# q of the first four pairs loaded in two DMAs of 2 KB rows, and a planner fed with traced landing times

## The chip, the cores and the metric

The kernel runs on one core of one Trainium2 chip. The metric is the device time of one execution in microseconds (us). The time before is the median of three runs.

## The reference

The inputs are q, k and v of shape (8, 8, 576, 64) (batch, heads, positions, head size) and two weights, w_in (512 x 2048) and w_out (2048 x 512), all fp32. The first half is retention, which is attention without a softmax and with a decay that depends on the head:

```python
scores = scale * np.matmul(q, k.transpose(0, 1, 3, 2))
gamma = 1.0 - 2.0 ** (-5.0 - np.arange(H, dtype=np.float32))
Dmat = np.where(rel >= 0, gamma[:, None, None] ** rel[None, :, :], 0.0)
ret = scores * Dmat[None, :, :, :]
return np.matmul(ret, v).astype(np.float32)
```

The second half takes the result as 4608 tokens of 512 and computes relu(x @ w_in) squared, times w_out. The output is 4608 x 512 in fp32.

## The kernel before

**Tiles.** The work is cut into 36 units of 128 tokens (all heads): 32 full ones (one batch entry, one chunk c of 128 positions) and four tail ones, which put the last 64 positions of two batch entries together. Two units make a group, so there are 18 groups. Each group has a retention part and a feed-forward part. Retention of a chunk is computed as scores inside the chunk (psc, masked into rx or rT), sums of k and v (psS) that go into a running state R, and an output psO, which takes the masked scores and the state of the chunk before. The decay is put into v (vdec), into R (dec128) and into the output (gam_full). The result is xT, in fp16. The feed-forward part multiplies xT with w_in into ph (L876), takes relu (rl) and square (gT) on ScalarE or VectorE, and multiplies gT with w_out into po. From group 1 on this second product is done by Strassen's scheme: seven half-size products (L973) over sums gS of gT (L946, VectorE) and differences wT of w_out (L827, VectorE). Group 0 uses w_out as it is (L916).

**The first four pairs.** Units 0 to 7 (PAIRED = 8) are handled as pairs of 256 positions of one batch entry. For these k, q and v are each loaded in one DMA (add_load_pair, L308) into a tile "pair" of 128 partitions, 8 heads and 128 numbers; a partition holds two consecutive positions (e = 0, 1), so that a row in memory has 2 x 64 fp32 numbers, 512 bytes. The casts to fp16 (L424; for v L420, with the decay) bring e out again, TensorE transposes k and q in blocks (psT, L439), and ScalarE or VectorE copy them to kqT (L450). Which engine casts what is set at L411. Positions of even and odd number sit apart in kqT, so the mask of the pairs (mask2, L211) and the product that forms xT (L577) are indexed by e. The later units load q in rows of 1 KB (L298) and are transposed by a DMA.

**The front.** FIRST (L240) sets the order of the first transfers: k0, q0, v0, k2, q2, v2, then the eight weight blocks w0 to w3 (w_in) and w4 to w7 (w_out), then k4, q4, v4, k6, q6, v6. The pair loads are issued by SyncE. The weight blocks are issued by GpSimd (L331), which casts them to fp16 on the way: the first issue waits for v0 to land, and the load of k4 waits for w5. The tile of a pair load comes from the pool "stage" (tag "wst", four buffers), which also holds gS. Until the first ph, TensorE has little to do; a list of 34 matmuls on zeros ("warm", WARM at L225) fills what the planner sees as idle time.

**The order of the work.** Every piece of work is a task with an engine, a key (priority), a duration, dependencies and resources. Schedule.emit (L42) plays these through in modelled time: each engine takes the ready task of the lowest key, and the order in which the tasks start is the order in which instructions are written into the engines' queues. On the chip each engine then works in this fixed order and waits on semaphores. The durations and landing times in the model thus cost nothing themselves, but they set the order. LAG holds extra landing time of single transfers (k4 and q4 only). BESIDE is a longer duration for the second half of a sum that is expected to collide with GpSimd. The constants of the tail units are made by tail_pool (L275), whose gate is tied to the cast of unit 4; unit 4 is one of a pair and has no such gate, so they are made at the very start.

Of the kernel before, what the change touches and what calls it, by code (L numbers as in the profile page):

```python
# [15 lines left out]
class Schedule:  # L16
# [7 lines left out]
    def add(self, eng, key, dur, fn, deps=(), acq=(), after=None, lag=0.0):  # L24
        t = dict(eng=eng, key=key, dur=dur, fn=fn, acq=acq, n=len(self.tasks), users=[], free=[], lag=lag,
                 left=len(deps), ready=0.0, lat=self.LAT[eng] if after is None else after)
        for d in deps:
            d["users"].append(t)
        self.tasks.append(t)
        return t  # L30
# [11 lines left out]
    def emit(self):  # L42
        ready = {e: [] for e in self.LAT}
        busy = {e: False for e in self.LAT}
        events = []
        order = []
        seq = 0

        def push(at, what, t):
            nonlocal seq  # L50
            seq += 1
            heapq.heappush(events, (at, seq, what, t))
        for t in self.tasks:
            if t["left"] == 0:
                heapq.heappush(ready[t["eng"]], (t["key"], t["n"], t))
        now = 0.0
        while True:
            for e in ready:
                if busy[e]:
                    continue  # L60
                held = []
                while ready[e]:
                    item = heapq.heappop(ready[e])
                    t = item[2]
                    if all(self.count[r] >= t["acq"].count(r) for r in t["acq"]):
                        for r in t["acq"]:
                            self.count[r] -= 1
                        t["start"] = now
                        order.append(t)
                        busy[e] = True  # L70
                        push(now + t["dur"], "end", t)
                        break
                    held.append(item)
                for item in held:
                    heapq.heappush(ready[e], item)
            if not events:
                break
            now = events[0][0]
            while events and events[0][0] <= now + 1e-9:
                _, _, what, t = heapq.heappop(events)  # L80
                if what == "end":
                    busy[t["eng"]] = False
                    for w in t["users"]:
# [20 lines left out]
def kernel(  # L104
# [9 lines left out]
    nc = tc.nc  # L114
# [96 lines left out]
    mask2 = const.tile([P, 2, 2, 64], FP32, name="mask2")  # L211
    nc.gpsimd.memset(mask2, 1.0)
    for c in range(2):
        for e in range(2):
            m = mask2[c * 64:(c + 1) * 64, e]
            nc.gpsimd.affine_select(out=m, in_=m, compare_op=ALU.is_ge, fill=0.0, base=-e, pattern=[[1, 2], [2, 64]],  # L216
                                    channel_multiplier=-2)
# [12 lines left out]
    BESIDE = 1.1  # L230
# [6 lines left out]
    LAG = {"k4": 0.7, "q4": 0.5}  # L237
# [37 lines left out]
    tail_pool = add_gated("POOL", 4, "v", 2.2, make_tail_pool)  # L275
# [32 lines left out]
    def add_load_pair(name, u):  # L308
        n = "kqv".index(name)

        def fn():
            if name != "q":
                tile_of["stage", u] = stage.tile([P, 2, H, 2 * D], FP32, name="pair", tag="wst")
            x = tile_of[name + "32", u] = tile_of["stage", u][:, n % 2]
            b, c = units[u][1:]
            t = nc.sync.dma_start(out=x, in_=(k, q, v)[n][b, :, c * P:(c + 2) * P, :].rearrange("h (p e) d -> p h (e d)", e=2))
            if (name, u) == ("k", 4):
                behind(t, tile_of["w", 5])
            tile_of["load", name, u] = t
        loaded[name, u] = loaded[name, u + 1] = dma_task(0, 1.81 if loaded else 2.9, fn, acq=("wst",) if name != "q" else (),  # L320
# [4 lines left out]
    def add_weight(i):  # L325
# [10 lines left out]
        t = add("SP", 0, 2.75, lambda: None, deps=last_load + [issue], after=2.1 + LAG.get(f"w{i}", 0.0))  # L336
# [25 lines left out]
    def half(x):  # L362
        return slice(64 * x, 64 * x + 64)
# [39 lines left out]
    def add_unit_pair(u, base):  # L403
# [4 lines left out]
        for i, name in enumerate("kqv"):  # L408
            xs[name] = []
            for e in range(2):  # L410
                eng = ("DVE" if (e if name == "v" else lead) else "ACT" if name == "k" and u >= 4 or u == 2 and e else  # L411
                       "DVE" if name == "q" and u == 2 else "POOL")

                def fc(name=name, e=e, eng=eng):
# [4 lines left out]
                    if name == "v":  # L419
                        (nc.vector if eng == "DVE" else nc.gpsimd).tensor_tensor(  # L420
                            out=t.rearrange("p (h d) -> p h d", d=D), in0=x,
                            in1=vdec[f"pair{e}"].rearrange("p (h o) -> p h o", o=1).to_broadcast([P, H, D]), op=ALU.mult)
                    else:
# [10 lines left out]
        for i, name in enumerate("kq"):  # L434
# [9 lines left out]
            for s in range(2):  # L444
                on_act = i == 0 or s == 0 or u > 0

                def fe(i=i, s=s, on_act=on_act):
                    if i == 0:
                        tile_of["kqT", u + s] = work.tile([P, 2 * NP, P], FP16, name="kqT", tag="kqT", bufs=6)
                    (nc.scalar.copy if on_act else nc.vector.tensor_copy)(  # L450
                        out=tile_of["kqT", u + s][:, i * NP:(i + 1) * NP].rearrange("p x (e t) -> p e x t", e=2),
                        in_=tile_of["psT", u, i][:, :, :, half(s)])
# [15 lines left out]
    def add_ret_pair(g):  # L468
# [7 lines left out]
        for e in range(2):  # L476
# [11 lines left out]
            for a in range(2):  # L488
                def fm(e=e, a=a):
                    nc.vector.tensor_tensor(  # L490
                        out=rT[e][:, a], in0=rT["ps", e][a].rearrange("p (n i) -> p n i", i=P),
                        in1=mask2[:, e].rearrange("p (o e) i -> p o (e i)", o=1).to_broadcast([P, NP, P]), op=ALU.mult)
# [208 lines left out]
    def after_sums(g, t, key, res):  # L701
# [24 lines left out]
        r2 = add("DVE", key + 0.3, 0.65, fr2, deps=[r1], acq=("R",))  # L726
# [95 lines left out]
    def add_wT(i, in0, in1):  # L822
        ts = []
        for h in range(2):
# [3 lines left out]
            ts.append(add("DVE", WT_KEY + i, 0.7, f, deps=sum((wcast[j] for j in range(4, 8 if i else 6)), [])))  # L828
# [6 lines left out]
    for x, y in ((t2, t1), (t4, t2)):  # L835
        for p in y:
            for w in x:
                sched.need(w, p)
# [19 lines left out]
    def add_ff(g):  # L858
# [10 lines left out]
        for fb in range(NF // nf):  # L869
# [18 lines left out]
            def fg(fb=fb, on_act=on_act):  # L888
# [43 lines left out]
    def add_strassen(g, us, base, sq):  # L932
# [7 lines left out]
        def add_sum(k, key, parts, in0, in1, op, deps, start=()):  # L940
            out_ = []
            for h in range(parts):
# [4 lines left out]
                out_.append(add("DVE", key + h, (BESIDE if h else 0.5) if parts > 1 else 0.8, f, deps=deps(h, parts) + list(start)))  # L947
# [164 lines left out]
```

## Time and profile before

| | before |
|---|---|
| median of 3 runs | 289.68 us (289.43 to 289.87) |
| span of the profiled execution | 288.5 us |
| TensorE matmul busy | 280.7 us |
| ScalarE busy | 187.5 us |
| VectorE busy | 177.7 us |
| GpSimd busy | 87.1 us |
| read from memory, written | 36.70 MB, 9.44 MB |
| share of ph (L876) in the chain that ended last | 43% |
| share of po (L973) in it | 36% |
| share of the DMA of w_in in it | 3% |

The profile is of one execution. Busy time is the time in which an engine works on an instruction; matmuls are pipelined, so a busy TensorE isn't always at its peak. The chain that ended last is followed back from the last instruction, at each step to what released it. In the profile's names PE is TensorE (PEld its weight loads), DVE is VectorE, ACT is ScalarE, POOL is GpSimd and SP is SyncE.

### The profile page before, as it was taken

Reading aid. Unit: us, or ns where it says so; the run is one execution under the profiler, and the core shown is the slowest. Engines: PE = TensorE matmul, PEld = TensorE weight load, DVE = VectorE, ACT = ScalarE, POOL = GpSimd, SP = SyncE. Lnnn points to the kernel's source line nnn. Section 1 sums busy time; section 2 is a strip of 40 time slices with the busy share of each in tenths; the row PEclk is TensorE's granted clock in tenths of the full one; section 3 lists DMA queues with packets and bytes.
Section 4 is the critical chain, followed back from the end, with each engine's and each line's share of the span. In section 5 each row is a group of like instructions: output and inputs, shape, how many; then the busy total and the mean of one; then the engine's idle time right before and its main releaser. Section 6 shows DMA issues by size and latency. Waiting matters only on the chain.

```text
span 288.5 us, 10135 instructions
## 1 busy us (share of the span) xinstructions
PE 280.7 (97%) x4346; PEld 236.0 (82%) x4346; DVE 177.7 (62%) x341; ACT 187.5 (65%) x363; POOL 87.1 (30%) x124
## 2 busy tenths in 40 slices
PE   7999999999999999999999999999999999999994
PEld 2568767888888888888888888888888888888883
DVE  3772389868466756657666574767666566364632
ACT  5558975667584757667575748675848665847830
POOL 5660045433525243423325151534433100000000
PEclk9999999999999999999999999999999999999999
DMA  7999999999999898989898997989899420102004
GB/s 202 275 208 206 248 277 267 168 240 144 212 222 186 210 201 216 179 214 168 222 146 197 231 185 182 220 200 248 177 160 228 110 75 5 73 2 75 0 2 145
DMA packets 122156, 49.94 MB, mean 173 GB/s; under 512 B 94720, under 2 KB 117760, under 8 KB 122112
## 3 DMA queue, kind: packets, MB, share of 16 engines
q1 hardware_dynamic: 117568, 44.84, 71.0%
q0 software_dynamic: 4224, 4.19, 8.8%
q8 instruction: 34, 0.56, 0.8%
q10 hardware_dynamic: 320, 0.26, 0.4%
q14 instruction: 10, 0.08, 0.1%
HBM read 36.70 MB, written 9.44 MB: 160 GB/s over the span
## 4 chain that ended last, share of the span: by engine, by line
PE 88%; DMA 3%; DVE 3%; POOL 2%; issue 2%; DVEq 0%; POOLq 0%
PE ph L876 43%; PE po L973 36%; PE psO L357 4%; DMA w_in<-in_moe_w_in_dram 3%; PE po L916 2%; PE psS L357 2%; PE psc L357 2%; DVE rx L490 1%; DVE o L996 1%; DVE gS L946 1%; POOL mask L216 0%; DVE vx L420 0%; POOL vx L420 0%; POOL w_in L331 0%; PE psT L439 0%
## 5 line engine op out<-in xcount | busy, mean ns | idle before, releaser
L876 PE MATMUL ph<-xT,w_in 128*128 128x256 f16 x1152 | 136.6, 273 | 0.3 <-DMA w_in<-in_moe_w_in_dram 0.3
L876 PEld LDWEIGHTS <-w_in 128*128 128x128 f16 x1152 | 111.4, 98 | 14.7 <-DMA w_in<-in_moe_w_in_dram 0.6
L884 ACT ACTIVATE rl<-ph 128x512 f16<-128x512 f32 x144 | 84.3, 586 | 50.7 <-PE ph L876 48.1
L894 ACT ACTIVATE gT<-rl 128x512 f16<-128x512 f16 x118 | 74.4, 631 | 3.4
L973 PEld LDWEIGHTS <-gS 128*128 128x128 f16 x544 | 51.7, 98 | 6.5
L973 PE MATMUL po<-wT,gS 128*128 128x256 f16 x408 | 55.8, 273 | 0.0
L946 DVE TENSOR_TENSOR gS<-gT,gS 128x512 f16<-128x512 f16 (+1 forms) x51 | 31.3, 613 | 24.2 <-ACT gT L894 23.7
L973 PEld LDWEIGHTS <-gT 128*128 128x128 f16 x408 | 39.6, 98 | 4.8
L973 PE MATMUL po<-w_out,gT 128*128 128x256 f16 x272 | 36.8, 273 | 0.0
L387 POOL TENSOR_TENSOR v<-v,vdec_full 128x512 f16<-128x512 f32 x24 | 26.6, 1108 | 28.1 <-DMA v<-in_v_dram 24.4
L371 POOL CAST kq<-k 128x512 f16<-128x512 f32 x28 | 19.7, 702 | 36.9 <-DMA k<-in_k_dram 31.2
L946 DVE TENSOR_TENSOR gS<-gT 128x1024 f16<-128x1024 f16 x34 | 24.7, 726 | 6.4 <-ACT gT L894 6.3
L382 POOL CAST kq<-q 128x512 f16<-128x512 f32 x24 | 15.6, 649 | 32.0 <-DMA q<-in_q_dram 31.8
L896 DVE TENSOR_TENSOR gT<-rl 128x512 f16<-128x512 f16 x26 | 11.8, 455 | 20.1 <-ACT rl L884 20.1
L996 DVE TENSOR_TENSOR o<-po,u 128x256 f32<-128x256 f32 x33 | 13.9, 422 | 15.3 <-PE po L973 7.7
L986 ACT COPY u<-po 128x256 f32<-128x256 f32 x34 | 12.5, 368 | 15.7 <-PE po L973 15.5
L751 DVE TENSOR_TENSOR xT<-psO,gam_full 128x512 f16<-128x512 f32 x28 | 18.0, 685 | 3.8 <-PE psO L357 3.6
L996 DVE TENSOR_TENSOR o<-po,p 128x256 f32<-128x256 f32 x18 | 7.6, 424 | 20.6 <-ACT u L986 12.7
L973 PE MATMUL po<-w_out,gS 128*128 128x256 f16 x136 | 18.0, 273 | 0.0
L692 DVE TENSOR_TENSOR rT<-psc,mask_full 128x512 f16<-128x512 f32 x24 | 15.6, 685 | 3.7 <-PE psc L357 3.2
L973 PE MATMUL po<-wT,gT 128*128 128x256 f16 x136 | 17.6, 273 | 0.0
L1047 ACT COPY o<-po 128x256 f32<-128x256 f32 x16 | 5.9, 370 | 10.8 <-PE po L973 9.1
(82 smaller groups left out, 227.1 us busy)
## 6 DMA issues: line engine op xcount, KB each, us to landing
out_dram<-o SPq DMA_DIRECT2D x32, 256.0 KB, 3.0
k<-in_k_dram SPq DMA_DIRECT2D x24, 256.0 KB, 4.5
q<-in_q_dram SPq DMA_DIRECT2D x96, 64.0 KB, 3.2
v<-in_v_dram SPq DMA_DIRECT2D x24, 256.0 KB, 3.5
pair<-in_k_dram SPq DMA_DIRECT2D x4, 512.0 KB, 7.0
pair<-in_q_dram SPq DMA_DIRECT2D x4, 512.0 KB, 6.1
pair<-in_v_dram SPq DMA_DIRECT2D x4, 512.0 KB, 6.6
w_in<-in_moe_w_in_dram POOLq DMA_DIRECT2D x4, 512.0 KB, 9.2
```

The lines of the kernel that those rows point to most:

```text
L357: t = nc.tensor.matmul(out_, lhsT=lhsT, rhs=rhs, start=start, stop=True, skip_group_check=True, tile_position=(64 * row, 64 * col))
L371: op(out=out_.rearrange("p (n b a d) -> p n b a d", n=2, b=2, a=2), in_=in_.rearrange("p (a n b) d -> p n b a d", n=2, a=2))
L382: nc.gpsimd.tensor_copy(out=tile_of["kq", u][:, 1].rearrange("p (t a d) -> p a t d", t=4, a=2), in_=tile_of["q32", u].rearrange("p (a t) d ...
L387: nc.gpsimd.tensor_tensor(out=t, in0=tile_of["v32", u], in1=vdec[kind].rearrange("p (h o) -> p h o", o=1).to_broadcast([P, H, D]), op=ALU. ...
L692: tile_of["masking", g] = nc.vector.tensor_tensor(out=tile_of["rT", g][:, :, a], in0=tile_of["psc", g][a].rearrange("p (s n i) -> p s n i" ...
L751: nc.vector.tensor_tensor(out=tile_of["x", g].rearrange("p n (s e i) -> p e (n s) i", s=n, e=2)[:, c], in0=y.rearrange("p (o t r) -> p o r ...
L876: nc.tensor.matmul(tile_of["ph", g, fb][:, j, :], lhsT=w_in16[:, m, fi * P:(fi + 1) * P], rhs=tile_of["x", g][:, m, :], start=(m == 0), st ...
L884: nc.scalar.activation(out=t, in_=tile_of["ph", g, fb], func=ACTF.Relu)
L894: nc.scalar.activation(out=t, in_=rl, func=ACTF.Square)
L946: nc.vector.tensor_tensor(out=tile_of["S", g][:, k, sl], in0=in0(sl), in1=in1(sl), op=op)
L973: nc.tensor.matmul(tile_of["pb", g, bank], lhsT=left(i), rhs=right[:, i, :], start=(start and i == 0), stop=(i == HF - 1), skip_group_chec ...
L996: nc.vector.tensor_tensor(out=o_tile(u)[:, half * HM:(half + 1) * HM], in0=bank(x), in1=tile_of[name, g], op=ALU.add)
```

## The change

It has four parts. First, q of each of the four pairs is loaded in two DMAs (heads 0 to 3 and 4 to 7), where a partition takes eight consecutive positions of one head, so that a row in memory has 2 KB. The positions then lie in another order, which the q casts, the copies to kqT, mask2 and the product for xT follow: position 8r + t of a chunk in place of 2i + e. Second, the two casts of k and the two of q in the pair of units 2 and 3 all go to ScalarE, and the tail's constants are tied to unit 8. Third, the planner gets landing times as traced (LAG for 13 transfers, 3.0 in place of 2.1 us for the weights, 2.58 in place of 2.75 us for each one's place in the stream, 1.41 in place of 1.81 for q). Fourth, the planner learns that some VectorE operations ("soft") run slowly while GpSimd works on something longer than 0.5 us (rate SHARED = 0.22), with shorter durations for these when they run alone; the halves of wT depend only on the halves they read; and HURRY brings forward the last relu, the squares on VectorE and the sums of group 1. The number of fillers, 34, is not changed by the diff.

```diff
@@ the planner
+    SHARED = 0.22
-    def add(self, eng, key, dur, fn, deps=(), acq=(), after=None, lag=0.0):
+    def add(self, eng, key, dur, fn, deps=(), acq=(), after=None, lag=0.0, soft=False):
...
+        def shared(beside):
+            t = port["task"]
+            if t is not None:
+                port["left"] -= (now - port["at"]) * (self.SHARED if port["beside"] else 1.0)
+                port["at"] = now
+                t["end"] = now + max(port["left"], 0.0) / (self.SHARED if beside else 1.0)
+                push(t["end"], "end", t)
+            port["beside"] = beside
...
+                        if e == "POOL" and t["dur"] > 0.5:
+                            shared(True)
...
@@ constants
-    mask2 = const.tile([P, 2, 2, 64], FP32, name="mask2")
+    mask2 = const.tile([P, 2, 8, 16], FP32, name="mask2")
...
-    BESIDE = 1.1
+    HURRY = 60
-    LAG = {"k4": 0.7, "q4": 0.5}
+    LAG = {"k0": 0.3, "q0": 0.6, "v0": 0.3, "k2": 0.2, "q2": 0.5, "v2": 1.0, "w2": 0.7, "w7": 1.4, "k4": 0.3, "q4": 1.1, "v4": 0.9, "q6": 0.8, "v6": 0.2}
-    tail_pool = add_gated("POOL", 4, "v", 2.2, make_tail_pool)
+    tail_pool = add_gated("POOL", 8, "v", 0.45, make_tail_pool)
@@ loads
-            t = nc.sync.dma_start(out=x, in_=(k, q, v)[n][b, :, c * P:(c + 2) * P, :].rearrange("h (p e) d -> p h (e d)", e=2))
+            src = (k, q, v)[n][b, :, c * P:(c + 2) * P, :]
+            if name == "q":
+                for a in range(2):
+                    t = nc.sync.dma_start(out=x[:, NP * a:NP * a + NP].rearrange("p t d -> p (t d)"),
+                                          in_=src.rearrange("(a x) (r t) d -> a r x (t d)", a=2, t=8)[a])
+            else:
+                t = nc.sync.dma_start(out=x, in_=src.rearrange("h (p e) d -> p h (e d)", e=2))
-        loaded[name, u] = loaded[name, u + 1] = dma_task(0, 1.81 if loaded else 2.9, fn, acq=("wst",) if name != "q" else (),
+        loaded[name, u] = loaded[name, u + 1] = dma_task(0, 2.9 if not loaded else 1.41 if name == "q" else 1.81, fn, acq=("wst",) if name != "q" else (),
-        t = add("SP", 0, 2.75, lambda: None, deps=last_load + [issue], after=2.1 + LAG.get(f"w{i}", 0.0))
+        t = add("SP", 0, 2.58, lambda: None, deps=last_load + [issue], after=3.0 + LAG.get(f"w{i}", 0.0))
@@ casts, copies, products of a pair
-                eng = ("DVE" if (e if name == "v" else lead) else "ACT" if name == "k" and u >= 4 or u == 2 and e else
-                       "DVE" if name == "q" and u == 2 else "POOL")
+                eng = ("DVE" if (e if name == "v" else lead) else "ACT" if name == "k" and u >= 4 or u == 2 and name != "v" else "POOL")
+                    elif name == "q":
+                        x = tile_of["q32", u].rearrange("p (a t) (s d) -> p a (t s) d", a=2, s=2)[:, :, NP * e:NP * e + NP]
+                        engines[eng](out=t.rearrange("p (t a d) -> p a t d", t=NP, a=2), in_=x)
...
+                        out_ = out_.rearrange("p x (t r) -> p t x r", r=16)
+                        in_ = in_.rearrange("p e y (r x) -> p (e y) x r", x=NP)[:, :, :, 16 * s:16 * s + 16]
...
-                    out=tile_of["x", g][:, :, s * P:(s + 1) * P].rearrange("p n (i e) -> p n e i", e=2),
-                    in0=tile_of["psO", g][s].rearrange("p (n e i) -> p n e i", n=NP, e=2),
-                    in1=gam_f.rearrange("p n (i e) -> p n e i", e=2), op=ALU.mult)
+                    out=tile_of["x", g][:, :, s * P:(s + 1) * P].rearrange("p n (r t) -> p n r t", t=8),
+                    in0=tile_of["psO", g][s].rearrange("p (n t r) -> p n r t", n=NP, t=8),
+                    in1=gam_f.rearrange("p n (r t) -> p n r t", t=8), op=ALU.mult)
@@ state, wT, squares, sums
-        r2 = add("DVE", key + 0.3, 0.65, fr2, deps=[r1], acq=("R",))
+        r2 = add("DVE", key + 0.3, 0.62, fr2, deps=[r1], acq=("R",), soft=True)
-            ts.append(add("DVE", WT_KEY + i, 0.7, f, deps=sum((wcast[j] for j in range(4, 8 if i else 6)), [])))
+            ts.append(add("DVE", WT_KEY + i, 0.68, f, deps=wcast[4 + h] + (wcast[6 + h] if i else []), soft=True))
-            r = add("ACT", place(4 * fb + 4), 0.6, fr, deps=[f1[-1]], acq=("rl",))
+            r = add("ACT", place(4 * fb + 4) - HURRY * (g == 1 and fb == 7), 0.6, fr, deps=[f1[-1]], acq=("rl",))
-            sq.append(add("ACT" if on_act else "DVE", place(4 * fb + 6), 0.63 if on_act else 0.55, fg, deps=[r] + sq[:1],
-                          acq=() if fb else ("g",)))
+            sq.append(add("ACT" if on_act else "DVE", place(4 * fb + 6) - HURRY * (g == 1 and not on_act), 0.63 if on_act else 0.43, fg, deps=[r] + sq[:1],
+                          acq=() if fb else ("g",), soft=not on_act))
-                out_.append(add("DVE", key + h, (BESIDE if h else 0.5) if parts > 1 else 0.8, f, deps=deps(h, parts) + list(start)))
+                out_.append(add("DVE", key + h - HURRY * (g == 1), 0.43 if parts > 1 else 0.72, f, deps=deps(h, parts) + list(start), soft=True))
```

More of the change, by code (lines that the diff above doesn't have):

```diff
@@ L22, in __init__ @@
         self.tasks = []
-    def add(self, eng, key, dur, fn, deps=(), acq=(), after=None, lag=0.0):
-        t = dict(eng=eng, key=key, dur=dur, fn=fn, acq=acq, n=len(self.tasks), users=[], free=[], lag=lag,
+    SHARED = 0.22
+    def add(self, eng, key, dur, fn, deps=(), acq=(), after=None, lag=0.0, soft=False):
+        t = dict(soft=soft, eng=eng, key=key, dur=dur, fn=fn, acq=acq, n=len(self.tasks), users=[], free=[], lag=lag,
                  left=len(deps), ready=0.0, lat=self.LAT[eng] if after is None else after)
@@ L56, in emit @@
         now = 0.0
+        port = dict(task=None, left=0.0, at=0.0, beside=False)
+        def shared(beside):
[6 more added lines that the diff above has]
+            port["beside"] = beside
         while True:
@@ L70, in emit @@
                         busy[e] = True
-                        push(now + t["dur"], "end", t)
+                        t["end"] = now + t["dur"]
+                        if t["soft"]:
+                            port.update(task=t, left=t["dur"], at=now)
+                            shared(port["beside"])
+                        else:
+                            push(t["end"], "end", t)
+                        if e == "POOL" and t["dur"] > 0.5:
+                            shared(True)
                         break
@@ L81, in emit @@
                 if what == "end":
+                    if abs(t["end"] - now) > 1e-6:
+                        continue
+                    t["end"] = -1.0
                     busy[t["eng"]] = False
+                    if t["soft"]:
+                        port["task"] = None
+                    elif t["eng"] == "POOL" and t["dur"] > 0.5:
+                        shared(False)
                     for w in t["users"]:
@@ L215 @@
             m = mask2[c * 64:(c + 1) * 64, e]
-            nc.gpsimd.affine_select(out=m, in_=m, compare_op=ALU.is_ge, fill=0.0, base=-e, pattern=[[1, 2], [2, 64]],
+            nc.gpsimd.affine_select(out=m, in_=m, compare_op=ALU.is_ge, fill=0.0, base=-e, pattern=[[1, 8], [8, 16]],
                                     channel_multiplier=-2)
@@ L315, in fn @@
             b, c = units[u][1:]
-            t = nc.sync.dma_start(out=x, in_=(k, q, v)[n][b, :, c * P:(c + 2) * P, :].rearrange("h (p e) d -> p h (e d)", e=2))
+            src = (k, q, v)[n][b, :, c * P:(c + 2) * P, :]
[3 more added lines that the diff above has]
+                                          in_=src.rearrange("(a x) (r t) d -> a r x (t d)", a=2, t=8)[a])
+            else:
+                t = nc.sync.dma_start(out=x, in_=src.rearrange("h (p e) d -> p h (e d)", e=2))
             if (name, u) == ("k", 4):
@@ L449, in fe @@
                         tile_of["kqT", u + s] = work.tile([P, 2 * NP, P], FP16, name="kqT", tag="kqT", bufs=6)
-                    (nc.scalar.copy if on_act else nc.vector.tensor_copy)(
-                        out=tile_of["kqT", u + s][:, i * NP:(i + 1) * NP].rearrange("p x (e t) -> p e x t", e=2),
-                        in_=tile_of["psT", u, i][:, :, :, half(s)])
+                    out_, in_ = tile_of["kqT", u + s][:, i * NP:(i + 1) * NP], tile_of["psT", u, i]
+                    if i == 0:
+                        out_, in_ = out_.rearrange("p x (e t) -> p e x t", e=2), in_[:, :, :, half(s)]
+                    else:
+                        out_ = out_.rearrange("p x (t r) -> p t x r", r=16)
+                        in_ = in_.rearrange("p e y (r x) -> p (e y) x r", x=NP)[:, :, :, 16 * s:16 * s + 16]
+                    (nc.scalar.copy if on_act else nc.vector.tensor_copy)(out=out_, in_=in_)
                 es.append(add("ACT" if on_act else "DVE", base + 3 + i + s / 2, 0.66, fe, deps=[t] + T["kqT", u + s],
@@ L491, in fm @@
                         out=rT[e][:, a], in0=rT["ps", e][a].rearrange("p (n i) -> p n i", i=P),
-                        in1=mask2[:, e].rearrange("p (o e) i -> p o (e i)", o=1).to_broadcast([P, NP, P]), op=ALU.mult)
+                        in1=mask2[:, e].rearrange("p (o t) r -> p o (t r)", o=1).to_broadcast([P, NP, P]), op=ALU.mult)
                 ms.append(add("DVE", base + 5 + e, 0.66, fm, deps=[t] + ms))
@@ L835 @@
     for x, y in ((t2, t1), (t4, t2)):
-        for p in y:
-            for w in x:
-                sched.need(w, p)
+        for w, p in zip(x, y):
+            sched.need(w, p)
     wT_done = {7: t3, 6: t2, 5: t1, 4: t4}
```

## The prediction

> **What bounds the kernel now.** I read the page first, for the engines and the slices.
>
> ```profile
> PE 280.7 (97%) x4346; PEld 236.0 (82%) x4346; DVE 177.7 (62%) x341; ACT 187.5 (65%) x363; POOL 87.1 (30%) x124
> ...
> PE   7999999999999999999999999999999999999994
> ...
> DMA  7999999999999898989898997989899420102004
> ```
>
> TensorE is busy in 97% of the span, and no other engine passes 65%. The matmuls aren't changed in number or shape, so the time can only come from stretches in which TensorE waits, or does fillers. The slices show one such stretch at the front (the 7) and one at the end (the 4). The DMA row is near 9 from the second slice to the 32nd, so at the front the transfers are the suspect. The chain of waits, in order of time, says which transfer:
>
> ```profile
> 8.90 0.98 POOL w_in L331
> 9.95 0.99 POOL vx L420
> 10.94 8.99 DMA w_in<-in_moe_w_in_dram
> 19.97 1.48 PE ph L876 x12
> 21.46 0.68 PE psO L357 x40
> 22.24 0.31 PE psO L357 x8
> 22.54 5.78 PE ph L876 x52
> ```
>
> The second block of w_in, issued at 10.94 us, lands at 10.94 + 8.99 = 19.93, and the ph matmuls wait for it. Behind that the chain runs on TensorE almost without a break to 43. What happens before 19.93 matters only through this landing. TensorE by microsecond:
>
> ```profile
> 18.00:19.00 1.00, 1.00 (x12) 1.00 1.24 205
> 19.00:20.00 1.00, 0.68 (x7) 1.00 1.24 208
> 20.00:21.00 1.00, 1.00 (x10) 1.00 1.25 206
> ...
> 48.00:49.00 1.00, 0.92 (x52) 1.00 0.65 167
> 49.00:50.00 1.00, 0.69 (x27) 1.00 1.26 287
> 50.00:51.00 1.00, 1.00 (x35) 1.00 1.09 224
> ```
>
> Busy time is the second figure: 0.32 us is idle at 19 to 20 (this is the wait for w_in) and 0.31 us at 49 to 50, where psS waits for VectorE's vx. There is little more to win after 20 us than these two. Last, why w_in lands when it does. First the transfers of 5 to 9 us, then the queues in 12 to 13 us:
>
> ```profile
> DMA packets 2299, 1.16 MB, mean 290 GB/s; under 512 B 32, under 2 KB 2299, under 8 KB 2299
> ...
> q1 hardware_dynamic: 2299, 1.16, 119.7%
> ```
>
> ```profile
> q1 hardware_dynamic: 552, 0.28, 114.9%
> q0 software_dynamic: 9, 0.01, 5.4%
> ```
>
> The six loads of the first two pairs (k0, q0, v0, k2, q2, v2; 0.524 MB each, in rows of 512 B) go at 290 GB/s, 1.81 us each. The first weight block was issued at 8.89 us, yet only 9 packets of its queue had moved before 13 us: it stands behind the pair loads. From there the stream is full, and the blocks land at 17.43, 19.93 and 22.43, 2.5 us apart. So each microsecond saved in the pair loads brings every weight block forward by as much.
>
> **What the Trainium skill says.** "DMA: Bandwidth & Descriptors", section "Specifications", gives a fabric ceiling of 435 GB/s, and says that rows of 512 B already suffice for line rate. The trace disagrees on the second: 512 B rows go at 290 GB/s. For rows of 2 KB the trace has only the output stores: the window 58.5 to 59.5 us, with 191 packets of 1 KB and more of 214, moved 393 GB/s. The section "Queues, rings and completion order" has the engines alternate between queue rows; here the trace shows one queue after the other (552 packets against 9), and the trace decides. "SBUF — State Buffer", on which operations contend: a VectorE operation with two SBUF inputs shuts GpSimd's reads out, or is shut out. The trace agrees: wT (L827, two SBUF inputs) takes 0.684 us mostly, once 1.53 beside GpSimd. "TensorE: Matmul & The Clock Gate", part 1: the clock falls to half after some 3.4 us idle. Here the warm matmuls start 0.43 us apart until 5 us and 0.216 after, and the later clock is full.
>
> **The change, part by part.**
>
> 1. *q of a pair in two DMAs of 2 KB rows.* Per load 1024 packets of 512 B become 256 of 2 KB. Bounds: nothing won (1.81 us), or the skill's ceiling (0.524 MB / 435 GB/s = 1.21 us, an estimate). I take the 393 GB/s of the stores: 1.33 us, 0.47 less. q0 and q2 both stand ahead of the weights: 2 x 0.47 = 0.94, bounds 0 and 1.2. v0, whose landing releases the first weight issue, comes 0.47 earlier, so the issue moves from 8.89 to about 8.4, while the stream would come free at about 11.9; it waited 4 us in the queue before, 3.5 now, so it should still be the queue and not the issue that starts it. One more issue on SyncE costs about 0.5 us (0.47 to 0.57 for the first two), behind the queue of transfers that SyncE fills ahead of need. q4 and q6 win 0.47 each as well, behind the weights, so the loads of the second two pairs come 0.9 to 1.9 us earlier.
> 2. *What goes with the new order of positions.* q casts, mask product, kqT copies and xT product keep their element counts. xT now reads PSUM in another order (L577, 0.68 us an operation); the later xT at L751 reads in such an order already and takes 0.685 us. The q copies have runs of 16 instead of 64: ACT 0.59 us each, at worst some 0.2 more on each of eight, and only the two of pair 0 and two of pair 2 lie in the front, where xT (done 15.95) is 1.5 us ahead of the weights. Nothing.
> 3. *Casts of the second pair all on ScalarE.* 4 x 0.62 = 2.5 us from k2's landing (about 9.9) on, beside 4 x 0.59 of kqT copies: ACT ends about 15, where the last copy now ends at 16.27. It takes 0.62 us from GpSimd and 0.42 us from VectorE. The copies queued behind these casts feed psc, which can come about 1 us earlier, ahead of the first weights; ph no longer has to stand behind it.
> 4. *The tail's constants move* from 5.2 us to behind the cast of unit 8 (near 51 us). VectorE's first cast stood behind them: vdl_tail waited 2.54 us for GpSimd and ended at 5.95, k0 had landed at 4.99. Up to 0.8 us of head start for pair 0, hidden by the wait for weights; at 51 us 0.23 us more on a full VectorE.
> 5. *The planner's numbers* (landings, the shared port, HURRY, halves of wT): no instruction is added or removed; only the order changes. The weights are counted 0.9 to 2.3 us later than before, so psO, psc and fillers should fall into the holes that the trace really has. I count half of the two idle pieces, 0.3 us. The 34 fillers are 34 already (warm x34); they only move.
>
> Sum: 0.94 + 0.3 = 1.24 us less: 289.68 - 1.24 = 288.4.
>
> **The rivals.**
>
> *More (287.4).* The rows run at 435 GB/s (1.2 us), both idle pieces go (0.63), and psO of group 1 fits in the gap between the first two weight blocks (some 0.4): 2.2 less. For it: psc comes early enough. Against it: its four masks (4 x 0.68 on a VectorE that was 93% busy in 16 to 20 us) end about when the second block lands.
>
> *Hidden (289.2).* The first block is paced by its issue, so only v0's 0.47 us counts; or VectorE, busy 3.86, 4.00 and 3.93 us in the three stretches of 4 us from 44 to 56, has no room for work that comes earlier, and hands the gain back. Against it: the loads and weights that feed VectorE there move by as much as TensorE does, and wT can start half by half.
>
> *Slower (290.5).* The new order is planned on short durations (0.43 us for half sums, 1.1 before), so in-order queues could be held behind operations that come late; about 18 groups at 0.05 us each are 0.9 us. Or the fillers are used up early and the clock falls: 3.4 us at half speed is 1.7 us by the skill's window. Against it: over 70 to 254 us only pieces of about 0.1 us are idle, the same at each group, so the queue of matmuls is well filled, and the front has no hole near 3.4 us.
>
> **How the numbers follow.** Forecast 0.61, more 0.16, hidden 0.12, slower 0.11. Under 289.1 counts as faster, over 290.26 as slower. The forecast's own bounds (rows at 340 to 435 GB/s, idle half or all) stay under 289.1 nearly always, so faster is 0.61 + 0.16 less 0.01; same 0.13; slower 0.11. The range from 287.2 to 289.9 takes in the fastest case and the hidden one, and leaves out the slower one and little else.
>
> **What would show it.** q0 and q2 in some 1.3 us each; weight landings near 16.5, 19.0 and 21.5; the chain through the w_in landing, but about 0.9 us earlier; ph x52 or its like under way at 21.6; casts on ScalarE only at 10 us. Wrong, if the weights land as before, if idle TensorE between 20 and 60 us grows by more than 0.5 us, if a slice of the clock row shows less than 9, or if pieces of idle time appear in the steady groups after 70 us.

## Result and profile after

| | before | after |
|---|---|---|
| median (range), 6 runs each | 289.74 us (289.43 to 290.30) | 290.93 us (290.41 to 291.58) |
| span of the profiled execution | 288.5 us | 289.2 us |
| packets moved | 122156 | 119149 |

The changed kernel is slower: the ratio is 1.0039, with a 95% interval of 1.0022 to 1.0056. The forecast was 288.4 us, and its range ended at 289.9. A ratio, here and below, is taken over all executions of a run and those of the kernel before that were measured with it (medians 289.74 to 290.05 us), without the two that took over 1.5% more than the fastest of their kernel, so it isn't the quotient of the medians shown. The page of the changed kernel, slices of TensorE and its clock:

```profile
PE   7899999899999999999999999999999999999994
...
PEclk9999999999999999999999999999999999999999
```

The first 7 and the last 4 of the TensorE row are as before, and the clock row is full, so the clock is not the cause. What is new is the 8 in the eighth slice (50.6 to 57.8 us; the 8 in the second is at the front). TensorE by microsecond, in windows of the prediction and two more (columns: window, us of it, busy time with the count of instructions, clock, DMA share, GB/s):

```profile
19.00:20.00 1.00, 1.00 (x12) 1.00 1.25 208
...
49.00:50.00 1.00, 1.00 (x33) 1.00 1.09 236
50.00:51.00 1.00, 0.38 (x4) 1.00 0.86 292
51.00:52.00 1.00, 0.20 (x2) 1.00 0.48 108
```

Both idle pieces of before (19 to 20 and 49 to 50 us) are gone, as intended. A larger one has come: 0.62 + 0.80 us of idle time at 50 to 52, that is 1.4 us (1.6 us if the matmuls that stand around it are taken at their usual spacing, 0.109 us from start to start; waits of TensorE are given in this way below). The chain of waits, at the front and there:

```profile
16.71 0.75 PE warm L283 x3
17.47 0.35 PE psc L390 x16
17.82 3.16 PE ph L914 x28
...
50.24 0.23 POOL iota_pt L300
...
50.49 0.68 DVE vdl_tail L209
...
51.19 0.30 ACT vdec_tail L211
51.49 0.27 ACT u L1024
...
51.80 0.60 PE po L1011 x4
```

At the front the landing of a weight block is no longer in the chain; ph follows on fillers and psc. At 50 us the constants of the tail units, which are first used at 100.7 us (the cast of v of the first tail unit), hold TensorE: GpSimd makes iota_pt, VectorE waits for it and makes vdl_tail, ScalarE waits for that and makes vdec_tail, and the copy "u" behind it on ScalarE frees the PSUM that the next product po waits for. GpSimd itself is late because of a load. The cast ahead of iota_pt, v of unit 8, in order of time:

```profile
48.98 1.04 POOL L420 TENSOR_TENSOR v<-v,vdec_full 128x512 f16<-128x512 f32 x1 [1.11 <-DMA v<-in_v_dram]
```

GpSimd stood idle for 1.11 us until v landed. Planned were 47.85 us for this cast and 48.95 for iota_pt, which began at 49.96. The waits between 40 and 56 us say how long each queue stood (columns: waiting engine and line, releaser, total us, times, longest):

```profile
ACT vdec_tail L211 <- DVE vdl_tail L209: 4.3, 1, 4.3
...
DVE vdl_tail L209 <- POOL iota_pt L300: 1.6, 1, 1.6
...
PE po L1011 <- ACT u L1024: 1.4, 1, 1.4
```

Where the time went as a whole shows when TensorE's progress is laid over the clock. The table gives, to about 0.1 us, each moment less the TensorE work that has been issued by then (the same 266.6 us in all, without fillers, at a fixed price for each shape: 0.109 us for a matmul of 256 columns, 0.216 for 512, 0.056 for 128, and about 0.0125 for each of the small ones of 64 rows); less is further ahead.

| at us | 20 | 30 | 42 | 50 | 53 | 58 | 75 | 280 |
|---|---|---|---|---|---|---|---|---|
| before | 14.23 | 14.82 | 14.87 | 16.48 | 16.87 | 17.46 | 17.89 | 17.45 |
| after | 13.76 | 14.34 | 14.44 | 15.79 | 17.63 | 18.22 | 18.59 | 18.24 |

The changed kernel is 0.4 to 0.7 us ahead until 50 us, 0.8 behind at 53, and nothing changes from there to the end. The front won about half of the forecast 0.94 us, and one wait at 50 to 52 lost more than that. (The two executions in the profiles took 291.04 and 290.18 us, 0.9 apart; the medians are 1.2 apart.)

### The profile page after: what moved, and what is told of

Its sections match the earlier page's. It is cut to its first block, busy times and chain, and to the rows that moved or that the text cites. A ratio compares the mean times of both kernels' runs of the same rounds, so it can differ in the third digit from the quotient of the medians.

```text
span 289.2 us, 10141 instructions
## 1 busy us (share of the span) xinstructions
PE 280.4 (97%) x4346; PEld 235.7 (81%) x4346; DVE 179.3 (62%) x340; ACT 188.5 (65%) x365; POOL 85.8 (30%) x123
## 2 busy tenths in 40 slices
DMA packets 119149, 49.95 MB, mean 173 GB/s; under 512 B 94784, under 2 KB 113728, under 8 KB 119104
## 4 chain that ended last, share of the span: by engine, by line
PE 91%; POOL 2%; issue 2%; DMA 1%; ACT 1%; DVE 1%; SPq 0%; POOLq 0%; DVEq 0%
PE ph L914 43%; PE po L1011 35%; PE psO L390 4%; PE po L954 2%; PE psS L390 2%; PE psc L390 2%; DMA k<-in_k_dram 1%; PE warm L283 1%; PE psT L474 1%; ACT gT L932 0%; POOL mask L243 0%; ACT rl L922 0%; POOL vx L452 0%; POOL w_in L364 0%; DVE o L1034 0%
## 5 line engine op out<-in xcount | busy, mean ns | idle before, releaser
L984 DVE TENSOR_TENSOR gS<-gT,gS 128x512 f16<-128x512 f16 (+1 forms) x51 | 32.4, 636 | 22.9 <-ACT gT L932 22.4
L420 POOL TENSOR_TENSOR v<-v,vdec_full 128x512 f16<-128x512 f32 x24 | 25.4, 1058 | 21.4 <-DMA v<-in_v_dram 17.1
L984 DVE TENSOR_TENSOR gS<-gT 128x1024 f16<-128x1024 f16 x34 | 25.3, 744 | 6.9 <-ACT gT L932 6.9
L500 DVE TENSOR_TENSOR R<-stmp,dec 128x512 f16<-128x512 f32 (+1 forms) x18 | 13.2, 731 | 0.5
```

The source lines that it names most:

```text
L420: nc.gpsimd.tensor_tensor(out=t, in0=tile_of["v32", u], in1=vdec[kind].rearrange("p (h o) -> p h o", o=1).to_broadcast([P, H, D]), op=ALU. ...
L984: nc.vector.tensor_tensor(out=tile_of["S", g][:, k, sl], in0=in0(sl), in1=in1(sl), op=op)
```

## The experiments

**The theory.** The tail's constants are only where the fault shows. Its cause is the planner's timeline. The change counts a load of q 0.40 us shorter (four of them) and the place of a weight block 0.17 us shorter (eight): 4 x 0.40 + 8 x 0.17 = 2.96 us. Every later transfer is planned that much earlier. On the chip the first weight block landed 1.45 us earlier, the next two about 1.0, the last 0.24, and behind them little is left of it: at unit 12 the trace is 0.73 us earlier, at unit 16 it is 0.55 later. The issue of the DMA that transposes k and q of a unit, planned and traced (us):

| unit | before, planned | before, traced | after, planned | after, traced |
|---|---|---|---|---|
| 8 | 52.61 | 52.01 | 48.45 | 49.37 |
| 12 | 76.41 | 76.43 | 73.45 | 75.70 |
| 16 | 102.41 | 102.62 | 99.45 | 103.17 |

Before, the plan hit these three within 0.6 us. After, it is 0.9, 2.3 and 3.7 us early, so in-order queues take up work whose inputs come later. Rivals: the constants alone (where they stand is the fault); the casts of the second pair on ScalarE; the order of positions with its short runs.

**1 and 2. The constants elsewhere.** From the changed kernel, the constants back at the start (E1), or behind the cast of unit 12 (E2).

```diff
-    tail_pool = add_gated("POOL", 8, "v", 0.45, make_tail_pool)
+    tail_pool = add_gated("POOL", 4, "v", 2.2, make_tail_pool)
```

```diff
-    tail_pool = add_gated("POOL", 8, "v", 0.45, make_tail_pool)
+    tail_pool = add_gated("POOL", 12, "v", 0.45, make_tail_pool)
```

> The changed kernel with the tail constants back at the very start (gate line as before). Theory (tail): the 1.7 us in which TensorE waits from 50.1 to 51.8 us in the changed kernel come from the chain iota_pt on GpSimd, vdl_tail on VectorE, vdec_tail on ScalarE, which the planner put into the in-order queues ahead of a copy from po; here the wait falls under 0.5 us and the time to 289.2 to 289.8, 1.2 to 1.8 under the changed kernel. Rival (port): the planner's short durations keep VectorE late at 44 to 57 us whatever the constants do; the time stays at 290.5 or more. Rival (loads): the later landing of k, q and v of unit 8 holds TensorE; over 290.3.

> The changed kernel with the tail constants behind the cast of unit 12, where the plan has slack on all three engines. Theory (tail): as with the constants at the start, 289.2 to 289.8, since the three small operations cost about 0.2 us of VectorE and 0.3 us of ScalarE and nothing waits behind them for long. Rival (constants cost wherever they stand behind a cast of GpSimd): a new wait of over 1 us near 73 us, time over 290.3.

E1: 290.62 us, ratio 1.0023 (1.0007 to 1.0039), where I had expected 289.2 to 289.8. The wait at 50 to 52 is gone, but under half of the loss comes back, and the interval overlaps that of the changed kernel. Its trace (of a run of 292.20 us, above the median) has other waits of TensorE in place of it: 0.80 us at 47.6, whose end the profile puts down to nothing, 0.61 at 78.6 for a sum on VectorE, and 0.36 at 84.8 and 0.68 at 123.2 for transposed k and q. E2: 294.20, ratio 1.0109 (1.0075 to 1.0143): the rival came true, and not the theory. The chain of E2 shows the same wait, larger:

```profile
75.44 1.04 POOL v L420
...
76.69 0.23 POOL iota_pt L300
...
76.95 0.68 DVE vdl_tail L209
...
77.65 0.30 ACT vdec_tail L211
```

The transposing DMA of unit 12 was planned for 73.45 us, and its trace has it at 76.06; TensorE waits 3.3 us, from 77.1 to 80.4. So the place of the constants decides how much one wait costs; that a late operation in the queue costs anything there comes from the plan, as E5 and E12 will show. E1, whose interval stays above 1, rules out that the constants are the whole of it.

**3. The rows alone.** The kernel before with q in rows of 2 KB, and what goes with them, and nothing else of the change.

```diff
...
+                for a in range(2):
+                    t = nc.sync.dma_start(out=x[:, NP * a:NP * a + NP].rearrange("p t d -> p (t d)"),
+                                          in_=src.rearrange("(a x) (r t) d -> a r x (t d)", a=2, t=8)[a])
...
```

> The kernel before with the 2 KB rows of q and what goes with them (mask2, casts, copies, xT product) and nothing else: planner numbers, casts and constants as before. If the weight stream sets the front (my prediction), the second block of w_in lands near 19.0 us and the time falls by 0.5 to 1.0, to 288.8 to 289.3. Rival (front path): TensorE starts ph no earlier, since xT of group 0 and the scores of group 1 stand in the queue as planned; the gain is only the 0.3 to 0.5 us wait for w_in, 289.3 to 289.5. Rival: the two halves of q land later than the one load did, the first copies and masks slip, and nothing is won or 0.3 us lost, 289.7 to 290.1.

289.97, ratio 1.0007 (0.9991 to 1.0023): no gain to be seen. The w_in blocks landed at 15.81, 18.53 and 21.07, that is 1.4 to 1.6 us earlier, and TensorE was 0.3 us ahead at 28 to 38 us. The time is that of the last rival, and its reason holds in part: xT of group 0 ended at 16.79 (15.95 before). The chain of this run, whose 291.29 us lies above the median, shows how it was lost:

```profile
48.40 0.87 DVE gS L959
...
49.27 1.54 DVE vx L426
...
50.85 0.41 PE psS L363 x28
```

It is the chain of before (gS, vx, psS), but vx takes 1.54 us, where the chain of before has 1.03 for it, and psS starts at 50.85 (49.86 before). At the front of the changed kernel, where GpSimd only issues a weight block beside it, the same operation took 0.69 us. Here GpSimd's cast of v runs beside it (48.94 to 50.25 us), and vx reads two inputs from SBUF; that such an operation is shut out while GpSimd reads is what the Trainium skill's page "SBUF — State Buffer" says in "Who interferes with whom", and this run agrees.

**4. The casts.** E1, with the casts of units 2 and 3 on their engines of before.

```diff
-                       "DVE" if (e if name == "v" else lead) else "ACT" if name == "k" and u >= 4 or u == 2 and name != "v" else "POOL"
+                       "DVE" if (e if name == "v" else lead) else "ACT" if name == "k" and u >= 4 or u == 2 and e else
+                       "DVE" if name == "q" and u == 2 else "POOL"
```

> The changed kernel with the tail constants at the start and the casts of units 2 and 3 as before (one of k on GpSimd, one of q on VectorE). Theory (casts): four casts on ScalarE push the transposes of q and with them psO and xT of group 0 back; here xT of group 0 ends near 16.0 instead of 16.9 us, ph starts up to 0.8 us earlier, and the time is 0.3 to 0.8 below the run with only the constants moved. Rival: ph waits for the scores of group 1 and the fillers in the queue all the same; within 0.2 us of that run.

291.39, ratio 1.0044 (1.0022 to 1.0067). The casts on ScalarE are not what costs: without them the time doesn't fall, and xT of group 0 ends at 17.04, not near 16.0 as the theory had it. Behind 75 us TensorE waits three times for a transposing DMA, the longest in the chain:

```profile
104.56 0.77 POOL kq L404
...
105.35 4.90 DMA kqT<-kq
...
110.29 0.32 PE psc L390 x16
```

Nothing of the change touches this stage but the planner's numbers.

**5. One number moved back.** The changed kernel, with 2.2 us added to the planned length of the last pair load, v6. No operation is touched, and the constants stay behind unit 8. The planned issue of the transposing DMA moves from 48.45 to 51.85 (unit 8) and from 73.45 to 75.65 (unit 12).

```diff
+    SHIFT = 2.2
-        loaded[name, u] = loaded[name, u + 1] = dma_task(0, 2.9 if not loaded else 1.41 if name == "q" else 1.81, fn, acq=("wst",) if name != "q" else (),
+        loaded[name, u] = loaded[name, u + 1] = dma_task(0, 2.9 if not loaded else 1.41 if name == "q" else 1.81 + SHIFT * ((name, u) == ("v", 6)), fn, acq=("wst",) if name != "q" else (),
```

> The changed kernel with 2.2 us more planned for the last pair load (v of unit 6), so that the plan has every later load 2.2 us later; no instruction is added. Theory (timeline): the new numbers move the planned loads from unit 8 on 3.0 us forward, the chip only 0.7 to 1, so everything behind them is queued too early; with the shift the transposing DMA of unit 12 is planned at 75.65, where the chip had it (75.70), the wait behind the tail constants falls from 1.7 us to under 0.4, and the time to 288.9 to 289.7, 1.2 to 2.0 under the changed kernel. Rival (constants): wherever they stand behind a cast they cost over 1 us; the time stays at 290.4 or more. Rival (port): the stretch 44 to 57 us is held by VectorE and GpSimd in each other's way; 290 or more, with idle TensorE near 48 to 52 us of 1 us.

289.89, ratio 0.9994 (0.9976 to 1.0011). The time is a little above the range that I gave, but the whole 0.4% is back, with the constants where they are in the changed kernel. TensorE of this run in the two windows of the wait:

```profile
50.00:51.00 1.00, 1.00 (x19) 1.00 0.70 172
51.00:52.00 1.00, 1.00 (x24) 1.00 1.08 242
```

No idle time is left at 50 to 52.

**6 to 8. The same by other ways.** E6 is the changed kernel with the transfer times and LAG of before (2.1, 2.75 and 1.81 us). E7 is E4 with the shift, E8 is E1 with the shift.

```diff
-    LAG = {"k0": 0.3, "q0": 0.6, "v0": 0.3, "k2": 0.2, "q2": 0.5, "v2": 1.0, "w2": 0.7, "w7": 1.4, "k4": 0.3, "q4": 1.1, "v4": 0.9, "q6": 0.8, "v6": 0.2}
+    LAG = {"k4": 0.7, "q4": 0.5}
-        loaded[name, u] = loaded[name, u + 1] = dma_task(0, 2.9 if not loaded else 1.41 if name == "q" else 1.81, fn, acq=("wst",) if name != "q" else (),
+        loaded[name, u] = loaded[name, u + 1] = dma_task(0, 1.81 if loaded else 2.9, fn, acq=("wst",) if name != "q" else (),
-        t = add("SP", 0, 2.58, lambda: None, deps=last_load + [issue], after=3.0 + LAG.get(f"w{i}", 0.0))
+        t = add("SP", 0, 2.75, lambda: None, deps=last_load + [issue], after=2.1 + LAG.get(f"w{i}", 0.0))
```

> The changed kernel with the planner's transfer numbers as before (1.81 us for q, 2.75 and 2.1 us for the weights, LAG of k4 and q4 alone). Theory (timeline): the loads from unit 8 on are planned where the kernel before has them, the waits near 50 us and behind 75 us go; 289.0 to 289.8, although the front is planned on landings that are not the chip's. Rival: the landings as traced are worth more in the front than they cost behind it; over 290.5.

> The constants at the start, the casts of units 2 and 3 as before, and the plan's later loads 2.2 us later. Without the shift this kernel was 0.8 us ahead of the kernel before at 75 us and lost 1.9 us between 80 and 120 in waits of the scores for their transposed k and q. Theory (timeline): with the shift the scores are queued later, these waits fall under 0.5 us, and the lead stays: 288.7 to 289.4, faster than before. Rival (loads bound the middle): whoever comes earlier waits longer; 290 or more, with idle TensorE of over 1 us between 75 and 130.

> The constants at the start and the plan's later loads 2.2 us later, casts all on ScalarE as in the change. Theory (timeline): within 0.3 us of the run that has the shift alone, if the constants hurt only where the plan is early: 289.0 to 289.7. Theory (tail, on its own): below that run by 0.5 or more.

E6: 289.73, 0.9989 (0.9975 to 1.0004). E7: 290.01, 1.0000 (0.9984 to 1.0017), where the same kernel without the shift had 1.0044. E8: 289.64, 0.9990 (0.9977 to 1.0004), where the one without it had 1.0023. All three lose the slowdown. E7's lead over the kernel before, which I had expected to stay (288.7 to 289.4), doesn't show in its time. E8's profiled execution has no wait of TensorE over 0.3 us from 17 us on, and a span of 287.1 us; at 288.76 us it is the fastest of its 22.

**9. The front, aiming for more.** E8 with later planned landings of v0, k2 and q2, nearer to those of the changed kernel's trace.

```diff
-    LAG = {"k0": 0.3, "q0": 0.6, "v0": 0.3, "k2": 0.2, "q2": 0.5, "v2": 1.0, "w2": 0.7, "w7": 1.4, "k4": 0.3, "q4": 1.1, "v4": 0.9, "q6": 0.8, "v6": 0.2}
+    LAG = {"k0": 0.3, "q0": 0.6, "v0": 0.8, "k2": 0.6, "q2": 0.9, "v2": 1.0, "w2": 0.7, "w7": 1.4, "k4": 0.3, "q4": 1.1, "v4": 0.9, "q6": 0.8, "v6": 0.2}
```

> The run with the constants at the start and the later loads planned 2.2 us later, and now the landings of v0, k2 and q2 counted 0.4 to 0.5 us later too, nearer to where the changed kernel's trace has them (v0 about 8.9 against 8.4 planned). The plan then puts the copy of kqT ahead of vx on VectorE, psO of group 0 ahead of the transposes of q2, and ph ahead of the scores of group 1. Theory (front path): ph starts about 16.9 instead of 17.7 us and the time falls by 0.4 to 0.8 against the run without it (0.999 of the kernel before): ratio to the kernel before 0.9962 to 0.9976. Rival (weights or loads take it back): ratio 0.9985 to 1.0005, since the second block of w_in (18.9 us) or the loads of the middle hold TensorE all the same.

289.93, 0.9992 (0.9980 to 1.0005): the gain that I expected did not come. The chain at the front:

```profile
9.39 7.93 DMA w_in<-in_moe_w_in_dram
...
17.37 0.61 PE ph L915 x4
17.98 0.57 PE psc L391 x32
```

The path of group 0 did get shorter: xT ended at 15.96 us (16.53 in E8), and the psc that E8 has in front of ph stand behind it. But the first weight block landed only at 17.32 (16.73 in E8), and ph waited 0.5 us for it. So ph starts at 17.37 all the same, as in E8 (17.35): the rival in which the weights take it back, though with the first block and not the second. And a psc waits 0.70 us at 135.8, far behind the part that was edited.

**10. The other way round.** The kernel before, with rows of 512 B and every operation as before, and only the planner's transfer times of the change.

```diff
-    LAG = {"k4": 0.7, "q4": 0.5}
+    LAG = {"k0": 0.3, "q0": 0.6, "v0": 0.3, "k2": 0.2, "q2": 0.5, "v2": 1.0, "w2": 0.7, "w7": 1.4, "k4": 0.3, "q4": 1.1, "v4": 0.9, "q6": 0.8, "v6": 0.2}
-        loaded[name, u] = loaded[name, u + 1] = dma_task(0, 1.81 if loaded else 2.9, fn, acq=("wst",) if name != "q" else (),
+        loaded[name, u] = loaded[name, u + 1] = dma_task(0, 2.9 if not loaded else 1.41 if name == "q" else 1.81, fn, acq=("wst",) if name != "q" else (),
-        t = add("SP", 0, 2.75, lambda: None, deps=last_load + [issue], after=2.1 + LAG.get(f"w{i}", 0.0))
+        t = add("SP", 0, 2.58, lambda: None, deps=last_load + [issue], after=3.0 + LAG.get(f"w{i}", 0.0))
```

> The kernel before with the planner's new transfer numbers alone (1.41, 2.58 and 3.0 us, LAG of 13 transfers), q in rows of 512 B as before. Theory (timeline): the plan has the loads from unit 8 on 3 to 4 us earlier while the chip has them where they were, so in-order queues are filled too early: slower, ratio 1.003 to 1.010. Rival (the new numbers are right and only the constants hurt): 0.997 to 1.001.

294.95, ratio 1.0178 (1.0154 to 1.0202). These numbers alone cost 5.2 us, more than the 1.003 to 1.010 that I gave. Its trace has the transposing DMA of units 8, 12 and 16 at 52.27, 78.43 and 103.60, so the plan is 3.8 to 5.4 us early (48.45, 73.45, 98.25). Late is not as bad as early: E3 runs on the plan of before, its trace has the three at 49.51, 74.28 and 100.14, 2.1 to 3.1 us ahead of the plan, and its ratio leaves room for 0.2% of loss at most. The largest wait of TensorE is 2.25 us long, for the transposed k and q. Its chain holds no matmul for 27.7 us (58.25 to 85.94); the last part of it:

```profile
77.85 1.30 POOL v L387
...
79.29 0.62 POOL kq L371
79.91 0.25 SPq L400
...
80.22 1.65 SPq L301
...
81.99 3.91 DMA kqT<-kq
...
85.94 0.32 PE psc L357 x16
```

SPq is SyncE's queue. It holds loads (L298, L301) and transposing DMAs (L400) in one fixed order. A transposing DMA waits for GpSimd's casts, the casts wait for loads, and the next loads stand behind the transposing DMA. So lateness in one is handed on to the next: this is the reading that the chain supports. In the order of issue this can be counted without any time: the transposing DMA of unit 8 stands behind five loads of whole k, q or v (counted from unit 8 on) in the changed kernel, E1, E2, E4 and E10, and behind six in the kernel before and in E3, E5 to E9, E11 and E12; that of unit 10 behind eleven against twelve. All with five have ratios from 1.0023 to 1.0178, all with six from 0.9989 to 1.0009. The count goes with the ratios in all fourteen kernels; to move one load alone wasn't tried, so it is a mark of the early plan, and not shown to be the whole of its cost.

**11 and 12. The price of two parts.** E11 is E8 with q in rows of 512 B and the copies, casts and products of before. E12 is the kernel before with only the constants moved behind unit 8 (E1's diff, the other way round).

```diff
...
+            t = nc.sync.dma_start(out=x, in_=(k, q, v)[n][b, :, c * P:(c + 2) * P, :].rearrange("h (p e) d -> p h (e d)", e=2))
...
```

> The run with the constants at the start and the later loads planned 2.2 us later (0.999 of the kernel before), with q in rows of 512 B as before. Theory (2 KB rows win in the front once the plan is right): slower than that run by 0.3 to 0.9 us, ratio to the kernel before 1.000 to 1.002, first ph again bound by the landings of w_in. Rival (the rows are worth nothing by themselves): 0.9980 to 0.9995.

> The kernel before with the tail constants behind the cast of unit 8 and nothing else. Its plan has that cast at about 51.5 us and the constants at 52.6, about where the chip has the cast, so nothing should wait: ratio 0.998 to 1.002 (theory: the constants hurt only where the plan is early). Rival (they hurt behind any cast): over 1.003 and a wait of over 1 us near 53 us.

E11: 289.80, 1.0004 (0.9992 to 1.0016), against 0.9990 for E8: rows of 2 KB are worth some 0.1%, or 0.4 us, at the edge of what the runs can tell. E12: 289.89, 1.0009 (0.9999 to 1.0019): the constants behind unit 8 cost at most 0.2% where the plan isn't early.

No kernel here is surely faster than the one before. The best two, E6 and E8, are 0.1% faster, with intervals that reach past 1.

## Why the prediction was wrong

**Part 5 is the step that failed.** It said of the planner's numbers that "only the order changes", that "psO, psc and fillers should fall into the holes that the trace really has", and gave 0.3 us of gain. The holes were filled: both idle pieces of before are gone. But the order changed for the whole kernel, not for the front. I looked at the numbers for the weights, which are counted later at their landing ("0.9 to 2.3 us later than before"), and did not add up what the same lines do to the planned stream: 2.96 us earlier for all that comes behind it. Even of the weights the reading was wrong: with their shorter places in the stream the plan has the first block land at 16.73 us (16.80 before) and the fourth at 24.47 (25.05). E10 puts the price of these numbers on the old kernel at 5.2 us (ratio 1.0178). E5 takes the price off the new kernel with one number, and E6 by undoing them. The planner was given traced landings for the first 20 transfers, and was 0.9 to 3.7 us early at the units behind them.

**Part 4** counted the constants as "0.23 us more on a full VectorE". vdl_tail took 0.67 us, but that isn't what cost. The step left out what stands in line: VectorE's and ScalarE's queues are in order, vdl_tail waited 1.6 us for GpSimd, vdec_tail stood 4.3 us on ScalarE, and the copy u that TensorE needed was behind it. With a plan that fits the chip it costs at most 0.2% (E12), and in E5 no loss is seen.

**Part 1** had the weights' landings right in this trace, by another way than it said. The first three blocks landed at 15.98, 18.92 and 21.46 us, against 16.5, 19.0 and 21.5 forecast. But the pair loads did not come 0.47 us earlier each: q0 landed at 7.06 (6.78 before), and the first weight issue went from 8.89 to 9.19 in place of 8.4. q2 took 1.41 us from the landing of k2 to its own, near the 1.33 forecast; q0 won nothing. The pair loads ended only 0.3 us earlier, while the weights began 1.1 us earlier, beside them (last section). And there is luck in the match: in the ten traces with rows of 2 KB the first block landed between 15.81 and 17.32 us and the second between 18.51 and 19.81 (median 19.02); in the four with 512 B at 17.26 to 17.43 and 19.67 to 19.93.

The gain of 0.94 us is the mis-sized term of this part: 0.4 to 0.5 us reached TensorE. The first ph started at 17.75, as before (17.73), because now other work sets it. Up to 16.93 it is the path of group 0: v0 is later, VectorE's copy to kqT of q takes 0.68 us in the new order (0.42 before) and stands behind vx, and xT ends at 16.93 (15.95 before). From there to 17.8 it is TensorE's own order, in which three fillers and 16 psc stand ahead of ph (the chain in the section on the result). I had seen the path of group 0 as "1.5 us ahead of the weights", and took the copy's cost for ScalarE's alone (part 2: "Nothing"; at worst 0.2). The margin of 1.48 us (15.95 to 17.43) has become -0.95: the first block lands at 15.98, and xT ends at 16.93.

**Part 3** said that psc could come ahead of the first weights, so that ph needn't stand behind it. It didn't: the chain has psc from 17.47 to 17.82 and ph right behind it, while the block had landed at 15.98. What the casts themselves are worth isn't told: with them on ScalarE E1 and E8 have 1.0023 and 0.9990, without E4 and E7 have 1.0044 and 1.0000. Both pairs lean to the change, and the intervals overlap.

The prediction named idle time of TensorE between 20 and 60 us that grows by more than 0.5 us as a sign that it is wrong. It grew from one wait of 0.5 us to one of 1.6.

**The rivals.** "Slower (290.5)" was nearest in time and had the right kind of mechanism, "in-order queues could be held behind operations that come late". It put it down to short durations, in pieces of 0.05 us over all groups, or to the clock. The runs showed one wait of 1.6 us, from transfer times; E5 to E8 keep the short durations and have no loss. The argument that I held against it, that the steady groups have no large idle pieces, was about the old order, and the change makes a new one.

**What stays open.** E8's profiled execution has a span 1.4 us shorter than that of before, but it is the fastest of 22 that spread from 288.76 to 291.02, and the profiled one of before (290.18) is slower than its median; what sets the slower ones of E8 back wasn't traced. Why the same transfer numbers cost 5.2 us in the old kernel (E10) and some 1.4 in the new one (1.0039, against 0.9989 for E6) isn't shown; that the old kernel's plan was then early by more (3.8 to 5.4 us against 0.9 to 3.7) fits. Nor is it known whether numbers that fit all transfers, not the first 20, would win anything.

## What to carry to other kernels

When a change edits the numbers of a planner, compare the planned with the traced times at points far behind the edited ones, before anything else: a correct landing for the first transfers with too short a time for each of them moves everything that follows. In in-order queues an operation that nobody needs yet can stop three engines if it waits for something late, so ask what stands behind it and not how long it takes. And when the wait that binds a stage is shortened, measure the margin of the next path to the same instruction with the change's own costs in it.

## What the hardware showed

With rows of 2 KB in the stream, the weights no longer waited for the end of the pair loads. In the window of before from 12 to 13 us the pair loads had 552 packets and the weights 9. The queues of the changed kernel in the same window:

```profile
q0 software_dynamic: 127, 0.13, 77.6%
q1 hardware_dynamic: 231, 0.11, 45.8%
```

Here both are at work. The last packets of v2 went at 13.07 us (13.38 before), the first of the weights at 11.74 (12.86 before). That some of the 16 DMA engines are through with the pair loads earlier than others would explain it, but the packets of one engine weren't told apart, so this isn't shown.

A packet of 2 KB took 84 to 89 ns from 4 to 6.5 us and 87 to 115 ns from 8.5 to 11 (medians of half microseconds). At 84 ns, 16 engines would move 390 GB/s (an estimate from these figures), as much as the 393 GB/s of the stores. The load of q2 came near it, 0.524 MB in 1.41 us or 372 GB/s; q0 did not (1.76 us from the landing of k0 in E8, 1.79 before).

A copy of 128 x 512 from PSUM took 0.68 us on VectorE when it reads at a step of four numbers and writes runs of 16, and 0.42 us before, with runs of 64 on both sides:

```profile
9.60 0.68 DVE L491 COPY kqT<-psT 128x512 f16<-128x512 f16 x1
```

```profile
8.82 0.42 DVE L450 COPY kqT<-psT 128x512 f16<-128x512 f16 x1 [1.25 <-ACT kqT L450]
```

Whether the step or the short runs cost the time wasn't told apart. On ScalarE the mean stayed at 0.59.
